# Highway FFN after linear attention: x added on GpSimd, output as fp16 transposes in pairs, weights 0.5(w_h - I), pairwise query sums, whole-batch exps

## Chip, cores and metric

One core of one Trainium2 chip. The metric is device time in microseconds (us). Engines: PE = TensorE matmul, PEld = TensorE weight load, DVE = VectorE, ACT = ScalarE, POOL = GpSimd, SP = SyncE. Every kernel here ran once with a profile and some rounds without, in turn with the kernel before on the same chip. Runs of a higher time at a lower granted TensorE clock are marked slow. Results are right unless "wrong on purpose" is said.

## Reference, cut

```python
# q, k, v: (8 batches, 8 heads, 576, 64) fp32; 0.1 * randn
q_s = softmax(q, axis=-1)                  # over the head dimension
k_s = softmax(k, axis=2)                   # over the sequence
kv  = einsum('bhsd,bhse->bhde', k_s, v)
x   = einsum('bhsd,bhde->bhse', q_s, kv).transpose(0, 2, 1, 3).reshape(4608, 512)
H   = maximum(x @ w_h, 0)
T   = sigmoid(x @ w_t + b_t)
out = T * H + (1 - T) * x                  # (4608, 512) fp32
```

## The kernel before: the parts concerned

Work is issued by hand in numbered positions, eight for each batch. An engine's instructions are queued in the order of issue. x and the gated term g are kept transposed (features on partitions) as fp16; an output tile turns 128 tokens back and is copied out of PSUM as fp32. Names in the profile: `eq`, `ek` are exp(q), exp(k); `psk` is k^T v with the column of sums; `rz`, `kvn` its reciprocal and normalised form; `r` the query sums; `pq`, `qsT` the query transposes; `px`, `xT` the attention output; `pt`, `ph` the two FFN products; `dd` and `g` the blend; `nat`, `o` the output tiles.

```python
def cast_weight(n, k_, eng):               # w_h: four slices, POOL and ACT in turn
    o, i = w16[n][:, k_], w32[n][:, k_]
    eng.copy(o, i) if eng is nc.scalar else eng.tensor_copy(o, i)

def q_sums(b, a):                          # two halves of a batch
    h = slice(2 * a, 2 * a + 2)
    nc.vector.reduce_sum(qsum[b][:, :, h], eq[b][:, :, h, :], axis=AX.X)

def q_scale_p(b, n0, n1):                  # the "products": eq times 1/sum, on POOL
    e, r = eq[b][:, n0:n1], qsum[b][:, n0:n1]
    nc.gpsimd.tensor_mul(e, e, r.broadcast_to(list(e.shape)))

def carry(c, ob):                          # ... four matmuls x @ w_h into ps
    nc.vector.scalar_tensor_tensor(dd, ps, 0.0, xv(ob), op0=ALU.max, op1=ALU.subtract)

def blend(c, ob):                          # th = tanh: T = 0.5 (1 + th)
    nc.vector.scalar_tensor_tensor(gv(ob), th, 1.0, dd, op0=ALU.add, op1=ALU.mult)

def turn_block(t, k_, xs, us):             # x + 0.5 g, turned back by two matmuls
    mm(t[:, k_, :], xs, ident, True, False)
    mm(t[:, k_, :], us, half_i, False, True)
# out_tile: 4 turn_blocks = 8 matmuls for 512 columns of fp32 in PSUM, one copy
...
    if b > 2:
        s = p + {3: -2, 4: -4}.get(b, -5)              # p = 8 * (b - 1)
        at(s, E(exp_half, b, "q", 0))
        at(s + 1, E(exp_half, b, "q", 1), E(q_sums, b, 0))
        at(s + 2, E(q_sums, b, 1), E(q_recip, b))
        if b > 3:
            at(s + 2, E(q_scale_p, b, 0, 4))
            at(s + 3, E(q_scale_p, b, 4, N9))
        s = p + {3: 0, 4: 0}.get(b, -1)
        at(s, E(exp_half, b, "k", 0), E(cast_v, b, 0))         # v casts: POOL
        at(s + 1, E(exp_half, b, "k", 1), E(cast_v, b, 1))
```

The softmax here doesn't subtract the row's maximum and nothing guards it: scores larger than these inputs give would overflow.

Of the kernel before, what the change touches and what calls it, by code (L numbers as in the profile page):

```python
# [18 lines left out]
def kernel(  # L19
# [10 lines left out]
    nc = tc.nc  # L30
# [74 lines left out]

    def cast_weight(n, k_, eng):
        o, i = w16[n][:, k_], w32[n][:, k_]
        if eng is nc.scalar:
            eng.copy(o, i)
        else:  # L110
            eng.tensor_copy(o, i)

    for w in "qkv":
        load(0, w, [nc.sync, nc.sync])
# [35 lines left out]
    def exp_half(b, which, a):  # L150
# [6 lines left out]
            AF.Exp,  # L157
        )

    def cast_v(b, a, eng=None):  # L160
        (eng or nc.gpsimd).tensor_copy(  # L161
            v16s[b % 2][:, :, 2 * a : 2 * a + 2, 0:64],
            in32["v"][b][:, 2 * a : 2 * a + 2].rearrange("p c n d -> p n c d"),
        )
# [30 lines left out]
    def q_sums(b, a):  # L195
        if a == 0:
            qsum[b] = small.tile([P, N9, 4], FP32, tag="r32", name=f"r32_{b}")
        h = slice(2 * a, 2 * a + 2)
        nc.vector.reduce_sum(qsum[b][:, :, h], eq[b][:, :, h, :], axis=AX.X)  # L199

    NG = [(0, 4), (4, 8), (8, 9)]

# [88 lines left out]
    def carry(c, ob):  # L291
        xv = views(c)[0]
        ps = ps_ht.tile([P, 8, 64], FP32, tag="ht", name=f"ph_{c}_{ob}")
        for k_ in range(4):
            mm(ps, w16["h"][:, k_, ob * P : ob * P + P], xv(k_), k_ == 0, k_ == 3)
        dd = mo.tile([P, 8, 64], FP16, tag="dd", name=f"dd_{c}_{ob}")
        nc.vector.scalar_tensor_tensor(  # L297
            dd, ps, 0.0, xv(ob), op0=ALU.max, op1=ALU.subtract
        )
        live[c, ob] = (live[c, ob], dd)  # L300

# [5 lines left out]
        )  # L307


    o32 = {}  # L310
    rows = out.rearrange("(g p n) m -> g p n m", g=B // 2, n=N9)

    def turn_block(t, k_, xs, us):
        dst = t[:, k_, :]
        mm(dst, xs, ident, True, False)
        mm(dst, us, half_i, False, True)

    def flat(t):
        return t.rearrange("p k d -> p (k d)")

    def out_tile(g, n, spare=False):
        if n % 4 == 0:
            o32[g, n // 4] = og.tile([P, 4, 512], FP32, tag="o32", name=f"o32_{g}_{n}")
        ps, tag = (ps_q, "qx") if spare and n % 4 < 3 else (ps_nat, "nat")
        t = ps.tile([P, 4, P], FP32, tag=tag, name=f"nat_{g}_{n}")
        for k_ in range(4):
            turn_block(
                t, k_,
                xT[g][:, k_, n].rearrange("p b d -> p (b d)"),
                gT[g][:, k_, n].rearrange("p b d -> p (b d)"),  # L330
            )
        o = o32[g, n // 4][:, n % 4, :]
        if spare and n % 2:
            nc.vector.tensor_copy(o, flat(t))
        else:
            nc.scalar.copy(o, flat(t))  # L336
        if n % 4 == 3:
            i = n // 4
            nc.sync.dma_start(rows[g][:, 4 * i : 4 * i + 4, :], o32[g, i])


    rows9 = out.rearrange("(g p n) m -> n p g m", g=B // 2, n=N9)[NM]
# [30 lines left out]
    def at(p, *fs):  # L373
        events.setdefault(p, []).extend(fs)
# [8 lines left out]
    for c in range(1, B + 1):  # L383
        for ob in range(4):
            at(8 * c + 2 * ob + 2, E(blend, c, ob))

    for g in range(B // 2):
        p = 16 * (g + 1)
        if g < B // 2 - 1:
            for i in range(8):  # L390
                at(p + 2 + 2 * i, E(out_tile, g, i))
        else:
            for i in range(8):
                at(p + 1 + i // 2, E(out_tile, g, i, True))
    at(8 * B + 8, E(most9), E(last9))

    at(8, E(q_sums, 2, 1), E(q_recip, 2), E(cast_v, 2, 0), E(q_scale_p, 2, 0, 4))
# [3 lines left out]
    for b in range(2, B):  # L401
        p = 8 * (b - 1)
        if b > 2:
            s = p + {3: -2, 4: -4}.get(b, -5)
            at(s, E(exp_half, b, "q", 0))
            at(s + 1, E(exp_half, b, "q", 1), E(q_sums, b, 0))
            at(s + 2, E(q_sums, b, 1), E(q_recip, b))
            if b > 3:
                at(s + 2, E(q_scale_p, b, 0, 4))
                at(s + 3, E(q_scale_p, b, 4, N9))  # L410
            s = p + {3: 0, 4: 0}.get(b, -1)
            at(s, E(exp_half, b, "k", 0), E(cast_v, b, 0))
            at(s + 1, E(exp_half, b, "k", 1), E(cast_v, b, 1))
            if b == 3:
                at(p + 1, E(q_scale_p, b, 0, 4), E(q_scale_p, b, 4, N9))
        tr, kv, x = {
            2: ((4, 5, 5), (3, 4), (6, 7, 7)),
            3: ((4, 5, 5), (3, 4), (6, 7, 7)),
            4: ((2, 3, 4), (4, 5), (6, 6, 7)),
        }.get(b, ((2, 3, 4), (3, 4), (5, 6, 7)))  # L420
        for i in range(3):
            at(p + tr[i], E(q_trans, b, i))
        at(p + kv[0], E(kv_half, b, 0))
        at(p + kv[1], E(kv_half, b, 1), E(kv_norm, b))
        at(p + x[0], E(x_pair, b, 0))
        at(p + x[1], E(x_pair, b, 1))
        at(p + x[2], E(x_left, b))
# [3 lines left out]
    for f in [  # L431
# [24 lines left out]
        E(exp_half, 2, "q", 0),  # L456
        E(x_pair, 1, 0), E(x_pair, 1, 1), E(blend, 0, 3), E(x_left, 1),
        E(exp_half, 2, "q", 1), E(q_sums, 2, 0),
    ]:
        f()  # L460
    for p in range(8, 8 * (B + 1) + 1):
# [33 lines left out]
```

## Time and profile before

| | before |
|---|---|
| time, median of 3 runs | 141.33 us (141.2 to 141.46) |
| span of the profiled run | 139.3 us |
| busy: PE, DVE, ACT, POOL | 88%, 76%, 63%, 32% |
| chain that ended last | PE 50%, DVE 29%, ACT 5%, POOL 5% |

The page, the table of stretches, one turn of the chain and the costly groups are shown in the prediction. A "turn" below is the time from the reciprocal of one batch's query sums to that of the next. One group, by shape (line, engine, operation, out<-in, count; busy us, mean ns; idle before it and what ended that):

```profile
L111 POOL CAST w16h<-w32h 128x512 f16<-128x512 f32 x2 | 1.3, 676 | 7.4 <-DMA w32h<-in_moe_w_h_dram 7.4
```

POOL casts its two slices of w_h as soon as the load lands, at 21 us, and nobody waits.

### The profile page before, as it was taken

What the parts mean: (1) busy time and instruction counts of PE and PEld (TensorE: products, weight loads), DVE (VectorE), ACT (ScalarE), POOL (GpSimd) and SP (SyncE); (2) the same over time, 40 slices, a digit from 0 to 9 for tenths busy, and PEclk for the clock granted to TensorE, in tenths of its full rate; (3) what the DMA queues carried; (4) which work ended last, traced back from release to release, by engine and by line L of the source; (5) the groups of instructions that cost most, each with busy time, mean ns of one, the idle gap of its engine ahead of it and who ended that gap; (6) DMA issues with size and microseconds to landing.
All of it is one profiled execution on the core that took longest, in us unless ns stands there. A gap on an engine that the chain in (4) does not pass through costs nothing.

```text
span 139.3 us, 3531 instructions
## 1 busy us (share of the span) xinstructions
PE 122.2 (88%) x1477; PEld 66.4 (48%) x1477; DVE 106.4 (76%) x200; ACT 88.1 (63%) x126; POOL 44.5 (32%) x37
## 2 busy tenths in 40 slices
PE   4979999967978799969979999999899999999920
PEld 1335344432443355535644754565465455577610
DVE  1395289987998799996996889979977675667840
ACT  3651377719931998639978879769773745565310
POOL 2006003500395429049309701960592000000000
PEclk9999999999999999999999999999999999999997
DMA  4999999999999999935999999950061015077745
GB/s 144 370 388 409 396 387 410 412 412 406 411 412 401 411 410 407 411 132 191 287 412 404 300 328 404 401 224 0 5 261 47 0 75 226 0 285 301 296 159 168
DMA packets 16022, 40.06 MB, mean 288 GB/s; under 512 B 644, under 2 KB 1672, under 8 KB 14984
## 3 DMA queue, kind: packets, MB, share of 16 engines
q1 hardware_dynamic: 16008, 39.85, 74.8%
q8 instruction: 11, 0.18, 0.5%
q14 instruction: 3, 0.02, 0.0%
HBM read 30.41 MB, written 9.44 MB: 286 GB/s over the span
## 4 chain that ended last, share of the span: by engine, by line
PE 50%; DVE 29%; ACT 5%; POOL 5%; DMA 3%; issue 3%; SPq 0%; DVEq 0%; POOLq 0%
PE pt L59 14%; PE ph L59 13%; DVE r L199 12%; PE nat L59 8%; POOL eq L216 5%; PE pq L64 4%; DVE g L305 4%; PE psk L59 3%; DMA q<-in_q_dram 3%; DVE dd L297 3%; PE warm L59 3%; ACT eq L154 2%; DVE eq L212 2%; PE px L59 2%; DVE r L204 2%
## 5 line engine op out<-in xcount | busy, mean ns | idle before, releaser
L288 ACT ACTIVATE pt<-pt,bt 128x512 f32<-128x512 f32 x36 | 23.9, 665 | 29.3 <-PE pt L59 29.3
L216 POOL TENSOR_TENSOR eq<-eq,r 128x1024 f16<-128x1024 f16 (+1 forms) x12 | 25.6, 2153 | 30.2 <-DVE r L204 30.2
L59 PE MATMUL pt<-xT,w16t 128*128 128x512 f16 x128 | 33.3, 380 | 2.1 <-DVE xT L257 1.7
L59 PE MATMUL ph<-xT,w16h 128*128 128x512 f16 x128 | 32.8, 380 | 0.0
L297 DVE SCALAR_TENSOR_TENSOR dd<-ph,xT 128x512 f16<-128x512 f32 x32 | 21.8, 682 | 7.6 <-PE ph L59 7.5
L305 DVE SCALAR_TENSOR_TENSOR g<-pt,dd 128x512 f16<-128x512 f32 x36 | 24.5, 681 | 1.8
L199 DVE TENSOR_REDUCE r<-eq 128x18 f32<-128x1152 f16 x16 | 21.4, 1345 | 4.3 <-ACT eq L154 4.3
L161 POOL CAST v<-v 128x1152 f16<-128x1152 f32 x15 | 16.9, 1147 | 22.7 <-DMA v<-in_v_dram 20.9
L154 ACT ACTIVATE eq<-q 128x1152 f16<-128x1152 f32 x16 | 18.5, 1171 | 2.7 <-DMA q<-in_q_dram 2.7
L154 ACT ACTIVATE ek<-k 128x1152 f16<-128x1152 f32 x16 | 18.4, 1170 | 2.1 <-DMA k<-in_k_dram 2.1
L59 PEld LDWEIGHTS <-w16t 128*128 128x128 f16 x144 | 12.6, 97 | 13.3 <-issue 1.1
L59 PE MATMUL nat<-half_i,g 128*128 128x128 f16 x140 | 18.7, 219 | 0.0
L59 PEld LDWEIGHTS <-w16h 128*128 128x128 f16 x144 | 12.4, 98 | 11.8 <-issue 1.4
L336 ACT COPY o<-nat 128x512 f32<-128x512 f32 x28 | 16.6, 594 | 1.7 <-issue 1.1
L255 ACT CAST xT<-px 128x512 f16<-128x512 f32 x24 | 13.4, 593 | 6.3 <-PE px L59 6.2
L59 PE MATMUL nat<-ident,xT 128*128 128x128 f16 x128 | 17.3, 219 | 0.0
L59 PE MATMUL warm<-wide,ident 128*128 128x512 f16 x52 | 15.3, 444 | 1.9 <-DVE wide L140 1.9
L59 PEld LDWEIGHTS <-g 128*128 128x128 f16 x144 | 14.1, 98 | 3.8 <-DVE g L305 0.4
L233 DVE COPY qsT<-pq 128x1024 f16<-128x1024 f16 (+1 forms) x24 | 12.8, 553 | 3.2 <-PE pq L64 3.0
L59 PEld LDWEIGHTS <-xT 128*128 128x128 f16 x128 | 12.5, 98 | 5.5 <-issue 2.6
L64 PE MATMUL pq<-ident,eq 128*128 128x128 f16 x144 | 11.5, 219 | 2.5 <-POOL eq L216 1.4
L64 PEld LDWEIGHTS <-eq 128*128 128x128 f16 x144 | 8.9, 98 | 6.4 <-POOL eq L216 3.1
(43 smaller groups left out, 84.6 us busy)
## 6 DMA issues: line engine op xcount, KB each, us to landing
out_dram<-o SPq DMA_DIRECT2D x8, 1024.0 KB, 4.8
q<-in_q_dram SPq DMA_DIRECT2D x7, 1152.0 KB, 13.3
k<-in_k_dram SPq DMA_DIRECT2D x7, 1152.0 KB, 14.3
v<-in_v_dram SPq DMA_DIRECT2D x6, 1152.0 KB, 14.7
v<-in_v_dram SPq DMA_DIRECT2D x4, 576.0 KB, 10.7
q<-in_q_dram SPq DMA_DIRECT2D x2, 576.0 KB, 4.1
k<-in_k_dram SPq DMA_DIRECT2D x2, 576.0 KB, 7.1
w32t<-in_moe_w_t_dram SPq DMA_DIRECT2D x1, 1024.0 KB, 13.6
```

Of the source, the lines that this page charges most:

```text
L59: mm = lambda o, l, r, st, sp: nc.tensor.matmul(o, l, r, start=st, stop=sp, skip_group_check=True)
L64: nc.tensor.matmul(o, i, ident, is_transpose=True, start=True, stop=True, skip_group_check=True,)
L154: nc.scalar.activation(dst[b][:, :, 2 * a : 2 * a + 2, :], in32[which][b][:, 2 * a : 2 * a + 2].rearrange("p c n d -> p n c d"), AF.Exp,)
L161: (eng or nc.gpsimd).tensor_copy(v16s[b % 2][:, :, 2 * a : 2 * a + 2, 0:64], in32["v"][b][:, 2 * a : 2 * a + 2].rearrange("p c n d -> p n ...
L199: nc.vector.reduce_sum(qsum[b][:, :, h], eq[b][:, :, h, :], axis=AX.X)
L216: nc.gpsimd.tensor_mul(e, e, r.broadcast_to(list(e.shape)))
L233: nc.vector.tensor_copy(qsT[b][:, :, n0:n1, :], t[:, :, 0:w, :])
L255: nc.scalar.copy(dst, t[c])
L288: nc.scalar.activation(ps, ps, AF.Tanh, bias=bt2[:, ob : ob + 1], scale=0.5)
L297: nc.vector.scalar_tensor_tensor(dd, ps, 0.0, xv(ob), op0=ALU.max, op1=ALU.subtract)
L305: nc.vector.scalar_tensor_tensor(gv(ob), th, 1.0, dd, op0=ALU.add, op1=ALU.mult)
L336: nc.scalar.copy(o, flat(t))
```

## The change

Five parts. **Weights**: relu(h) - x = max(h, 0) - x is rewritten so that the matmul gives 0.5 (h - x), with 0.5 (w_h - I) as the weight; dd = max(-0.5 x, 0.5 (h - x)), and the 0.5 of the gate is in dd already. **x on POOL**: g + x is formed on POOL instead of by the second matmul of each block. **Pairs**: g + x is then one fp16 tensor, so an output tile is 4 transposes, two tiles share a PSUM bank, and one copy takes both. **Sums**: a batch's query sums by two halving fp16 adds and a short reduction, instead of two long reductions. **Exps**: one exp for a batch instead of two halves, for batches 3 to 7. PE loses 128 small matmuls; POOL gains 32 adds.

```diff
 def cast_weight(n, k_, eng):
+    d = slice(k_ * P, k_ * P + P)                       # for w_h only
+    nc.vector.tensor_sub(i[:, d], i[:, d], ident)
-    eng.copy(o, i) / eng.tensor_copy(o, i)
+    eng.mul(o, i, 0.5) / eng.tensor_scalar_mul(o, i, 0.5)
+def exp_all(b, which): ...                              # one activation, 2304 columns
+def q_sums_all(b):
+    nc.vector.tensor_add(t32, e[:, :, 0:32], e[:, :, 32:64])
+    nc.vector.tensor_add(t16, t32[:, :, 0:16], t32[:, :, 16:32])
+    nc.vector.reduce_sum(qsum[b].rearrange("p n c -> p (n c)"), t16, axis=AX.X)
-    dd, ps, 0.0, xv(ob), op0=ALU.max, op1=ALU.subtract
+    dd, xv(ob), -0.5, ps, op0=ALU.mult, op1=ALU.max
+def add_x(c, ob):
+    nc.gpsimd.tensor_add(gv(ob), gv(ob), xv(ob))
-def out_tile(g, n, ...): ...                            # 8 matmuls, fp32, 1 tile
+def out_pair(g, i, ...): ...                            # 8 transposes, fp16, 2 tiles, one copy
...
             at(8 * c + 2 * ob + 2, E(blend, c, ob))
+            if c < B:
+                at(8 * c + 2 * ob + 3, E(add_x, c, ob))
...
-                at(p + 2 + 2 * i, E(out_tile, g, i))    # p = 16 * (g + 1)
+                at(p + 3 + 4 * i, E(out_pair, g, i))
...
-            at(s, E(exp_half, b, "q", 0))
-            at(s + 1, E(exp_half, b, "q", 1), E(q_sums, b, 0))
-            at(s + 2, E(q_sums, b, 1), E(q_recip, b))
+            at(s, E(exp_all, b, "q"))
+            at(s + 1, E(q_sums_all, b))
+            at(s + 2, E(q_recip, b))
```

More of the change, by code (lines that the diff above doesn't have):

```diff
@@ L107, in cast_weight @@
         o, i = w16[n][:, k_], w32[n][:, k_]
+        if n == "t":
+            eng.tensor_copy(o, i)
+            return
+        d = slice(k_ * P, k_ * P + P)
+        nc.vector.tensor_sub(i[:, d], i[:, d], ident)
         if eng is nc.scalar:
-            eng.copy(o, i)
+            eng.mul(o, i, 0.5)
         else:
-            eng.tensor_copy(o, i)
+            eng.tensor_scalar_mul(o, i, 0.5)
     for w in "qkv":
@@ L158, in exp_half, with exp_all @@
         )
+    def exp_all(b, which):
+        dst, p_ = {"k": (ek, ekp), "q": (eq, eqp)}[which]
+        dst[b] = p_.tile([P, N9, 4, 64], FP16, tag="e", name=f"e{which}_{b}")
+        nc.scalar.activation(
+            dst[b], in32[which][b].rearrange("p c n d -> p n c d"), AF.Exp
+        )
     def cast_v(b, a, eng=None):
@@ L199, in q_sums @@
         nc.vector.reduce_sum(qsum[b][:, :, h], eq[b][:, :, h, :], axis=AX.X)
+    t32 = consts.tile([P, N9 * 4, 32], FP16, name="t32")
+    t16 = consts.tile([P, N9 * 4, 16], FP16, name="t16")
+    def q_sums_all(b):
+        qsum[b] = small.tile([P, N9, 4], FP32, tag="r32", name=f"r32_{b}")
+        e = eq[b].rearrange("p n c d -> p (n c) d")
+        nc.vector.tensor_add(t32, e[:, :, 0:32], e[:, :, 32:64])
+        nc.vector.tensor_add(t16, t32[:, :, 0:16], t32[:, :, 16:32])
+        nc.vector.reduce_sum(
+            qsum[b].rearrange("p n c -> p (n c)"), t16, axis=AX.X
+        )
     NG = [(0, 4), (4, 8), (8, 9)]
@@ L307, in blend @@
         )
+    def add_x(c, ob):
+        xv, gv = views(c)
+        nc.gpsimd.tensor_add(gv(ob), gv(ob), xv(ob))
     o32 = {}
@@ L315, in turn_block, with out_pair @@
         mm(dst, xs, ident, True, False)
-        mm(dst, us, half_i, False, True)
+        mm(dst, us, ident, False, True)
     def flat(t):
         return t.rearrange("p k d -> p (k d)")
-    def out_tile(g, n, spare=False):
-        if n % 4 == 0:
-            o32[g, n // 4] = og.tile([P, 4, 512], FP32, tag="o32", name=f"o32_{g}_{n}")
-        ps, tag = (ps_q, "qx") if spare and n % 4 < 3 else (ps_nat, "nat")
-        t = ps.tile([P, 4, P], FP32, tag=tag, name=f"nat_{g}_{n}")
-        for k_ in range(4):
-            turn_block(
-                t, k_,
-                xT[g][:, k_, n].rearrange("p b d -> p (b d)"),
-                gT[g][:, k_, n].rearrange("p b d -> p (b d)"),
-            )
-        o = o32[g, n // 4][:, n % 4, :]
-        if spare and n % 2:
-            nc.vector.tensor_copy(o, flat(t))
-        else:
-            nc.scalar.copy(o, flat(t))
-        if n % 4 == 3:
-            i = n // 4
-            nc.sync.dma_start(rows[g][:, 4 * i : 4 * i + 4, :], o32[g, i])
+    def out_pair(g, i, spare=False):
+        if i % 2 == 0:
+            o32[g, i // 2] = og.tile([P, 4, 512], FP32, tag="o32", name=f"o32_{g}_{i}")
+        ps, tag = (ps_q, "qx") if spare and i < 3 else (ps_nat, "nat")
+        t = ps.tile([P, 2, 512], FP16, tag=tag, name=f"nat_{g}_{i}")
+        for j in range(2):
+            for k_ in range(4):
+                ptrans(
+                    t[:, j, k_ * P : k_ * P + P],
+                    gT[g][:, k_, 2 * i + j].rearrange("p b d -> p (b d)"),
+                )
+        h = i // 2
+        o = o32[g, h][:, 2 * (i % 2) : 2 * (i % 2) + 2, :]
+        if spare and i % 2:
+            nc.vector.tensor_copy(o, t)
+        else:
+            nc.scalar.copy(o, t)
+        if i % 2:
+            nc.sync.dma_start(rows[g][:, 4 * h : 4 * h + 4, :], o32[g, h])
     rows9 = out.rearrange("(g p n) m -> n p g m", g=B // 2, n=N9)[NM]
@@ L385 @@
             at(8 * c + 2 * ob + 2, E(blend, c, ob))
+            if c < B:
+                at(8 * c + 2 * ob + 3, E(add_x, c, ob))
     for g in range(B // 2):
         p = 16 * (g + 1)
-        if g < B // 2 - 1:
-            for i in range(8):
-                at(p + 2 + 2 * i, E(out_tile, g, i))
-        else:
-            for i in range(8):
-                at(p + 1 + i // 2, E(out_tile, g, i, True))
+        for i in range(4):
+            if g < B // 2 - 1:
+                at(p + 3 + 4 * i, E(out_pair, g, i))
+            else:
+                at(p + 3 + i, E(out_pair, g, i, True))
     at(8 * B + 8, E(most9), E(last9))
@@ L411 @@
             s = p + {3: 0, 4: 0}.get(b, -1)
-            at(s, E(exp_half, b, "k", 0), E(cast_v, b, 0))
-            at(s + 1, E(exp_half, b, "k", 1), E(cast_v, b, 1))
+            at(s, E(exp_all, b, "k"), E(cast_v, b, 0))
+            at(s + 1, E(cast_v, b, 1))
             if b == 3:
@@ L458 @@
         E(exp_half, 2, "q", 1), E(q_sums, 2, 0),
+        *[E(add_x, 0, ob) for ob in range(4)],
     ]:
```

## The prediction

> **What bounds the kernel now.** I read, in this order: the page (busy shares, slices, chain shares), the table of stretches, the chain of waits in order of time, the groups by shape, and the timelines of VectorE (DVE), ScalarE (ACT) and GpSimd (POOL). The page names no single bound:
>
> ```profile
> span 139.3 us, 3531 instructions
> PE 122.2 (88%) x1477; PEld 66.4 (48%) x1477; DVE 106.4 (76%) x200; ACT 88.1 (63%) x126; POOL 44.5 (32%) x37
> PE 50%; DVE 29%; ACT 5%; POOL 5%; DMA 3%; issue 3%; SPq 0%; DVEq 0%; POOLq 0%
> ```
>
> The table of stretches shows why; its columns are PE, weight loads, DVE, ACT, POOL, granted clock, DMA share, GB/s:
>
> ```profile
> 20.00:30.00 10.00, 8.59 (x86) 4.40 (x85) 9.57 (x19) 5.24 (x7) 3.60 (x4) 1.00 1.04 412
> 90.00:100.00 10.00, 9.57 (x154) 5.42 (x152) 8.89 (x17) 8.15 (x13) 3.80 (x4) 1.00 0.25 101
> 110.00:120.00 10.00, 10.00 (x81) 5.46 (x78) 6.53 (x11) 5.71 (x11) 0.00 (x0) 1.00 0.26 105
> ```
>
> To about 62 us DVE sets the pace (9.57 of 10 us in 20 to 30), from 100 us PE alone does, and between them the two take turns. One turn of 12.57 us, in the chain of waits (start, us, what):
>
> ```profile
> 82.23 0.46 DVE kvn L188 x2
> 82.68 1.26 DVE r L199
> 83.94 0.60 DVE dd L297
> 84.54 1.27 DVE r L199
> 85.83 0.38 DVE r L204
> 86.21 0.55 DVE g L305
> 86.76 0.61 DVE xT L257
> 87.40 0.38 PE pt L59
> 87.78 0.45 PE nat L59 x8
> ...
> 92.16 0.41 PE psk L59 x36
> ...
> 94.09 0.48 PE psk L59 x36
> ```
>
> Seen here: 5.4 us of DVE (the normalised kv product, two query sums r, reciprocal, xT) and then 7.1 us of PE up to the second psk. An output tile (nat) costs PE 0.45 us. POOL is off this path and has large gaps, but not with much room: in POOL's timeline the first half of the v cast ends at 91.67 us, and the psk that reads it starts at 92.16.
>
> **What the Trainium skill says.**
> 1. "SBUF — State Buffer", section "Who interferes with whom": a DVE instruction with two SBUF inputs, or in a two-port mode, and a GpSimd instruction that reads SBUF exclude each other for a whole instruction. The trace agrees: the one DVE cast of v (39.96 us) fell across two POOL products and the second of these took 2777 ns, while the same shape at 51 us took 2330.
> 2. "GPSIMD Engine Reference", section 3.1: two-input work on GpSimd pays about 2.6 cycles an element, which at its 1.2 GHz is 2.2 ns. The trace shows 1900 ns for 1024 elements and 2330 for 1280: 1.7 to 1.9 ns each, a little better.
> 3. "VectorE: DVE Perf Modes", section "The perf-mode tier table": tensor_tensor runs 2x on 16-bit SBUF data, tensor_reduce only 1x. The trace: 692 and 824 ns for 1024 and 1280 elements (0.52 ns each plus 164), against 1345 ns for a sum over 1152.
> 4. "PSUM — Partial Sum Buffer", specifications: a transpose writes its input type into PSUM. So two tiles of 512 fp16 fit one 2 KiB bank. The query transposes already do this, 8 in 0.45 us, the same as 8 output matmuls.
>
> The groups that carry the costs:
>
> ```profile
> L216 POOL TENSOR_TENSOR eq<-eq,r 128x1280 f16<-128x1280 f16 x6 | 14.4, 2406 | 0.0
> L216 POOL TENSOR_TENSOR eq<-eq,r 128x1024 f16<-128x1024 f16 x6 | 11.4, 1900 | 30.2 <-DVE r L204 30.2
> L199 DVE TENSOR_REDUCE r<-eq 128x18 f32<-128x1152 f16 x16 | 21.4, 1345 | 4.3 <-ACT eq L154 4.3
> L336 ACT COPY o<-nat 128x512 f32<-128x512 f32 x28 | 16.6, 594 | 1.7 <-issue 1.1
> ```
>
> **The change, part by part.**
>
> *Output tiles.* 32 tiles of 8 matmuls become 16 pairs of 8 transposes: PE saves 16 x 0.45 = 7.2 us busy. ACT copies of 256, 384 and 512 elements took 372, 480 and 594 ns, so 1024 is about 1.03 us for a pair, against two of 0.59; little is gained. On the path the saving counts where PE is it: after the last psk (107.07 us) there are 14 tiles, which become 7 pairs: 7 x 0.45 = **-3.1 us**.
>
> *Query sums, batches 3 to 7.* By the slopes above: add of 1152 0.76 us, of 576 0.46 us, sum of 576 about 0.75 us; starts overlap by some 0.08, so 1.75 against 2.53 us: -0.78 us each, four of the five inside a turn. Both adds have two SBUF inputs, so they can be held by POOL.
>
> *Whole-batch exps.* Two took 2.22 us start to end; one should take some 2.1. About -0.1 each, but it holds tanh or an xT copy up to 1 us longer. Nothing on the path, save at batch 3 below.
>
> *x on POOL.* 32 adds of 512 elements, by the POOL slope about 1.0 us each: POOL goes from 44.5 to some 77 us busy. PE must now wait for the last add of a chunk before its first output pair. The dd and g operations keep their operand kinds and their 680 ns.
>
> *Weights.* Before the first carry DVE gets four 128x128 fp32 subtractions (about 0.3 us each), and ACT and POOL then scale the slices.
>
> Now along the path:
>
> *Start.* Before, w_h was cast at 21.3 to 22.6 us, beside DVE work, and the first dd started at 25.05. The order of the changed kernel puts the subtractions after the eq products, which end at 25.12. They end near 26, POOL's two scalings (676 ns each) and ACT's two near 27.1; only then comes the first ph's last quarter, and dd near 27.6. ACT's tanh stands behind its scalings too. The qsT copies and psk follow: I take **+2.2 us** (DVE idles a part of it, so not all 2.5).
>
> *Batch 3.* POOL's order becomes: add of chunk 1's last block, second half of the v cast, then the query products. The add waits for g (49.67 before), so the products start some 1.3 us later though the sum is earlier; the whole exp also delays an xT copy by 1 us. **+1.1.**
>
> *Batch 4.* Gain of the sum against POOL's longer row: **0.**
>
> *Batches 5 and 7.* This is the step I trust most. After the reciprocal POOL runs: products 4.2, add 1.0, v casts 2.2, and only then the add of the previous chunk's last block 1.0, so 8.5 us. PE runs pt, ph, pt, pq, ph and reaches the first pair of the new group 4.6 us after the reciprocal in batch 7 (86.21 to 87.78, plus 3 us, by the same spacing): it waits some 3.9 us. Then pair 0.45, pq 0.45, psk 0.41, pt 0.97, pq 0.11, psk 0.41: second psk done at 11.3, before at 8.3 (98.78 to 107.07): **+3.0** in batch 7. In batch 5 the same count gives 11.4 against 9.4, less the sum's saving of 0.7: **+1.3.**
>
> *Batch 6.* PE meets the v cast: products 4.2, add 1.0, half cast 1.1, so 6.4 against 5.5 without: the tiles' saving is eaten, the sum's stays, and its adds may wait for POOL adds: **+0.2.**
>
> *End.* The last pair is copied by DVE (about 1.2 us, by 424, 550 and 692 ns for 256, 384 and 512) between the last blends, and the last large store leaves about 2 us later relative to the last matmul, with 1 MB taking 4.8 us to land: **+0.5 to 1.**
>
> Sum: 2.2 + 1.1 + 0 + 1.3 + 0.2 + 3.0 - 3.1 + 0.7 = +5.4, so 146.7 us. I lean back from it, since every stall is estimated from one ordering and a tuned kernel may hide some: **145.5 us**.
>
> **Rivals.**
> 1. *The savings arrive, POOL stays hidden.* For: POOL was 32% busy, the added work is spread, and PE and DVE, which form 79% of the chain, both lose work. If only the start cost stays (+2) and each turn gets 1.5 us shorter (three turns), with -3.1 in the tail: 141.3 + 2 - 4.5 - 3.1 = about 136. Against: the POOL queue is in order, and the adds stand behind 6.4 us of products and casts.
> 2. *Gain and loss cancel.* The stalls of batches 5 and 7 are there, but the start is hidden and sums pay fully: 141.3 + 4.3 - 3.1 - 2.4 + 1 = about 141. For: the two largest terms are of equal size. Against: at the start DVE is busy 9.57 of 10 us.
> 3. *Worse than the sum.* The lock makes both adds of each sum wait for a POOL add (about 1 us each, five batches), and PE's pauses of 4 us lower its clock. 146.7 + 3 to 5 = about 151. The clock was 1.00 in all stretches but the end, so no run here shows how long a pause it stands.
>
> **Range and chances.** The cases weigh about 0.1, 0.25, 0.5 (my sum) and 0.15. The range is 141.0 to 150.0: a term off by one us in two or three places. Under 138.5 (faster by over 2%): 0.11. From 138.5 to 144.2: 0.27. Above: 0.62.
>
> **What would show it.** Start: the first dd near 27.6 instead of 25.05, with PE waiting for w16h on POOL or ACT. Batches 5 and 7: weight loads of g waiting 3 to 4 us for POOL's add, twice; in batch 3 well under that. POOL adds near 1.0 us, POOL near 77 us busy. Sum adds near 0.76 and 0.46 us, longer where they meet POOL. Tail: from the last psk to the last ph 21 us instead of 24. I am wrong if the POOL add runs in about half a microsecond, if PE reaches the pairs late anyway because DVE holds it, or if the start delay vanishes in a wait that I did not see.

## The result

The changed kernel took **155.58 us** (median of 4 runs, 155.31 to 158.48; the one of 158.48 is slow) against 141.28 before in the same rounds: ratio 1.1004, 95% interval 1.0978 to 1.103. A ratio is the mean time of one kernel's fast runs over that of the other's of the same rounds, so not quite the ratio of the medians. It was slower, as predicted, but by 14 us and not by 4: outside the stated range of 141 to 150.

The page of the kernel after, with the row of the granted clock in 40 slices:

```profile
span 153.3 us, 3294 instructions
PE 120.8 (79%) x1349; PEld 60.7 (40%) x1349; DVE 106.8 (70%) x207; ACT 86.1 (56%) x102; POOL 83.3 (54%) x69
PEclk9995999779999999999999699999999879999998
PE 35%; POOL 25%; DVE 20%; issue 7%; ACT 6%; DMA 3%; SPq 0%; POOLq 0%; DVEq 0%; ACTq 0%
```

No engine became the bound: none is busier than 79%. But POOL, 5% of the chain before, is 25% of it now. It is a wait for POOL and not its load. The clock fell in four places. PE saved only 1.4 us of busy time of the 7.2 that the fewer matmuls should give, as its other matmuls ran slower in those places (pt: 392 ns each in the mean, 380 before; ph 401 and 380).

Three stretches of after (the columns as in the prediction: PE, PEld, DVE, ACT, POOL, clock, DMA share, GB/s):

```profile
20.00:30.00 10.00, 5.78 (x27) 2.15 (x24) 7.72 (x17) 4.13 (x6) 2.60 (x2) 0.95 1.05 392
80.00:90.00 10.00, 7.67 (x51) 3.85 (x52) 6.41 (x15) 5.85 (x8) 8.50 (x7) 0.83 0.47 163
110.00:120.00 10.00, 5.01 (x41) 2.63 (x40) 6.35 (x13) 4.25 (x4) 8.84 (x7) 1.00 0.26 106
```

In 20 to 30 neither DVE (9.57 before) nor PE (8.59) is full. In 110 to 120, where PE had been busy without a gap, it is busy for half the time while POOL is busy for 8.84 us.

*Where the time went*, by milestones in the two traces (start times, us): the reciprocal of batch n's query sums is "recip n", that of the last psk "psk 7".

| up to | before | after | shift | added here | predicted |
|---|---|---|---|---|---|
| recip 1 | 22.86 | 24.83 | +2.0 | +2.0 | none |
| first dd | 25.05 | 31.65 | +6.6 | +4.6 | +2.2 (start) |
| recip 2 | 37.73 | 44.34 | +6.6 | 0 | |
| recip 4 | 60.43 | 68.70 | +8.3 | +1.7 | +1.1 (batch 3) |
| recip 5 | 72.25 | 81.73 | +9.5 | +1.2 | 0 (batch 4) |
| recip 6 | 85.83 | 97.09 | +11.3 | +1.8 | +1.3 (batch 5) |
| recip 7 | 98.40 | 110.62 | +12.2 | +1.0 | +0.2 (batch 6) |
| psk 7 | 107.12 | 123.74 | +16.6 | +4.4 | +3.0 (batch 7) |
| last dd | 131.12 | 145.29 | +14.2 | -2.4 | -3.1 (tail) |
| end of span | 139.3 | 153.3 | +14.0 | -0.2 | +0.7 |

*Start.* The chain of waits (start, us, what), first of before, then of after:

```profile
24.30 0.82 DVE eq L212
25.13 0.61 DVE dd L297
```

```profile
26.28 0.82 DVE eq L238
27.11 0.21 DVE w32h L113
27.40 3.13 POOL w16h L117 x2
30.58 2.36 PE ph L59 x6
```

Before, the first dd follows the DVE work directly. After, DVE's subtractions, then two scalings on POOL and the first ph, the latter at a low clock, stand between. The scalings ran in 1482 and 1665 ns, where the plain cast of the same shape took 676.

*A turn with the pairs at its beginning* (batch 7). POOL's timeline of before: products as soon as the reciprocal is there, then two v casts, and nothing else:

```profile
98.95 4.19 POOL L216 TENSOR_TENSOR eq<-eq,r 128x1024 f16<-128x1024 f16 x2 [6.20 <-DVE r L204]
103.09 2.24 POOL L161 CAST v<-v 128x1152 f16<-128x1152 f32 x2
```

Chain of after:

```profile
113.02 2.33 POOL eq L242
115.35 0.17 POOL g L338
...
116.40 2.23 POOL v L174 x2
118.64 1.12 POOL g L338
...
119.80 0.45 PE nat L64 x5
...
121.11 1.74 PE pt L59 x4
```

PE waits for the add of the last block of the previous chunk, which stands in POOL's queue behind products, another add and two v casts. PE's own timeline puts the pause at 3.06 us, and the next pt takes 1.74 us instead of 0.97: the clock fell.

*Query sums*, timeline of DVE (start, us, instruction, and in brackets the idle time before it), first of before, where kvn stands between the two halves:

```profile
68.42 1.34 DVE L199 TENSOR_REDUCE r<-eq 128x18 f32<-128x1152 f16 x1
...
70.47 0.49 DVE L188 TENSOR_TENSOR kvn<-psk,rz 128x128 f16<-128x128 f32 x2
70.88 1.34 DVE L199 TENSOR_REDUCE r<-eq 128x18 f32<-128x1152 f16 x1
```

Then of after, with two of POOL's adds of that time:

```profile
77.22 1.21 DVE L221 TENSOR_TENSOR t<-eq 128x1152 f16<-128x1152 f16 x1 [0.49 <-ACT eq L169]
78.47 1.29 DVE L222 TENSOR_TENSOR t<-t 128x576 f16<-128x576 f16 x1
...
81.13 0.23 DVE L199 RECIPROCAL rz<-psk 128x2 f32<-128x2 f32 x2
81.33 0.49 DVE L201 TENSOR_TENSOR kvn<-psk,rz 128x128 f16<-128x128 f32 x2
```

```profile
77.79 2.98 POOL L338 TENSOR_TENSOR g<-g,xT 128x512 f16<-128x512 f16 x2
```

Two things are seen. The adds last 1.21 and 1.29 us where 0.76 and 0.46 were predicted: POOL was at work. And batch 5's whole sum stands in DVE's queue *before* rz and kvn of batch 4, for which PE is waiting. Over the five batches, by shape:

```profile
L338 POOL TENSOR_TENSOR g<-g,xT 128x512 f16<-128x512 f16 x32 | 37.8, 1190 | 19.9 <-DVE g L331 19.8
L221 DVE TENSOR_TENSOR t<-eq 128x1152 f16<-128x1152 f16 x5 | 5.3, 1056 | 1.0 <-ACT eq L169 1.0
L222 DVE TENSOR_TENSOR t<-t 128x576 f16<-128x576 f16 x5 | 4.0, 791 | 0.2
```

### The profile page after: what moved, and what is told of

Same layout as the page of the kernel before. It is cut to its first block, busy times and chain, and to the rows that moved or that the text cites. A ratio compares the mean times of both kernels' runs of the same rounds, so it can differ in the third digit from the quotient of the medians.

```text
span 153.3 us, 3294 instructions
## 1 busy us (share of the span) xinstructions
PE 120.8 (79%) x1349; PEld 60.7 (40%) x1349; DVE 106.8 (70%) x207; ACT 86.1 (56%) x102; POOL 83.3 (54%) x69
## 4 chain that ended last, share of the span: by engine, by line
PE 35%; POOL 25%; DVE 20%; issue 7%; ACT 6%; DMA 3%; SPq 0%; POOLq 0%; DVEq 0%; ACTq 0%
POOL eq L242 12%; PE pt L59 10%; PE ph L59 10%; POOL g L338 5%; POOL v L174 5%; DVE r L212 4%; PE warm L59 3%; DMA q<-in_q_dram 3%; PE nat L64 3%; PE psk L59 3%; PE pq L64 3%; ACT eq L160 2%; PE px L59 2%; DVE t L221 2%; POOL w16h L117 2%
## 5 line engine op out<-in xcount | busy, mean ns | idle before, releaser
L338 POOL TENSOR_TENSOR g<-g,xT 128x512 f16<-128x512 f16 x32 | 37.8, 1190 | 19.9 <-DVE g L331 19.8
L59 PE MATMUL ph<-xT,w16h 128*128 128x512 f16 x128 | 35.3, 401 | 4.6 <-POOL w16h L117 4.6
L242 POOL TENSOR_TENSOR eq<-eq,r 128x1024 f16<-128x1024 f16 (+1 forms) x12 | 25.6, 2153 | 11.1 <-DVE r L230 7.4
L323 DVE SCALAR_TENSOR_TENSOR dd<-xT,ph 128x512 f16<-128x512 f16 x32 | 21.7, 678 | 9.9 <-PE ph L59 9.8
L368 ACT CAST o<-nat 128x1024 f32<-128x1024 f16 x14 | 14.2, 1012 | 14.0 <-PE nat L64 12.8
L64 PE MATMUL nat<-ident,g 128*128 128x128 f16 x128 | 10.9, 225 | 3.8 <-POOL g L338 3.7
L64 PEld LDWEIGHTS <-g 128*128 128x128 f16 x128 | 8.9, 101 | 8.5 <-POOL g L338 4.4
L212 DVE TENSOR_REDUCE r<-eq 128x18 f32<-128x1152 f16 x6 | 8.0, 1349 | 4.7 <-ACT eq L160 4.7
L169 ACT ACTIVATE eq<-q 128x2304 f16<-128x2304 f32 x5 | 10.6, 2128 | 0.0
L169 ACT ACTIVATE ek<-k 128x2304 f16<-128x2304 f32 x5 | 10.6, 2122 | 0.0
L117 POOL TENSOR_SCALAR w16h<-w32h 128x512 f16<-128x512 f32 x2 | 3.1, 1574 | 13.4 <-DVE w32h L113 13.4
## 6 DMA issues: line engine op xcount, KB each, us to landing
v<-in_v_dram SPq DMA_DIRECT2D x4, 576.0 KB, 11.3
```

The costliest lines, as they stand in the source:

```text
L59: mm = lambda o, l, r, st, sp: nc.tensor.matmul(o, l, r, start=st, stop=sp, skip_group_check=True)
L64: nc.tensor.matmul(o, i, ident, is_transpose=True, start=True, stop=True, skip_group_check=True,)
L169: nc.scalar.activation(dst[b], in32[which][b].rearrange("p c n d -> p n c d"), AF.Exp)
L323: nc.vector.scalar_tensor_tensor(dd, xv(ob), -0.5, ps, op0=ALU.mult, op1=ALU.max)
L338: nc.gpsimd.tensor_add(gv(ob), gv(ob), xv(ob))
L368: nc.scalar.copy(o, t)
```

## The experiments

Theory after the result: the cost is the *place in the queue* of the added work (adds ahead of v casts and products on POOL, weight work behind DVE's, a sum ahead of kvn). Rivals: the *amount* of POOL work and its holding of DVE; the fallen clock; the operations themselves. The first four runs add one part to the kernel before (141.3 us in the same rounds; 141.4 to 141.5 in the later ones).

| run | us, median | ratio to before (fast runs) |
|---|---|---|
| p1_weights | 147.93 | 1.0464 [1.0381, 1.0547] |
| p2_sums | 143.01 | 1.0117 [1.0100, 1.0134] |
| p3_exps | 141.59 | 1.0039 [0.9999, 1.0079] |
| p4_xpool (wrong) | 149.47; the fast one 146.15 | none: one fast run |
| u1_scale_dve | 154.66 | 1.0963 |
| u2_pairs_later | 152.86 | 1.0769 |
| u3_dead_add (wrong) | 150.59 | 1.0633 |
| u4_no_add (wrong) | 143.82; the fast one 140.37 | none: one fast run |
| v1_weights_early | 141.51 | 0.9995 [0.9958, 1.0031] |
| v2_sums_late | 142.19 | 1.0025 [0.9971, 1.0079] |
| v3_casts_first (wrong) | 139.24 | 0.9832 [0.9794, 0.9870] |
| v4_fill | 154.59 | 1.0889 |
| w2_v1_v3 | 140.26 | 0.9892 [0.9826, 0.9958] |
| w1_best | **136.39** | **0.9656 [0.9626, 0.9687]** |
| w4_add3_later | 137.67 | 0.9726 [0.9679, 0.9774] |
| w3_all_reordered | 140.42 | 0.9942 [0.9913, 0.9971] |

A caution: the profiles of after, p1, u2 and u4 have a dip of the clock during warm-up, ahead of everything that was changed, and reach recip 1 by 1.4 to 2.9 us later than before; those of u1, u3, v4 and the others have none. Whether a run without a profile has it, no trace shows. Where such runs are compared, the stretch from recip 1 to the last dd in the two profiles is given as well: 108.3 us in before, 120.5 in after.

### p1_weights: the weights part alone, on the kernel before

```diff
+        nc.vector.tensor_sub(i[:, d], i[:, d], ident)
+        eng.mul(o, i, 0.5) / eng.tensor_scalar_mul(o, i, 0.5)     # ACT / POOL
-            dd, ps, 0.0, xv(ob), op0=ALU.max, op1=ALU.subtract
+            dd, xv(ob), -0.5, ps, op0=ALU.mult, op1=ALU.max
-        mm(dst, us, half_i, False, True)
+        mm(dst, us, ident, False, True)
```

> The kernel before with one part of the change alone: weights 0.5(w_h - I), the new form of dd, and ident in place of half_i in the output matmuls. Right result. My theory: the start is paid in full and never won back, because the chain from 25 to 62 us is a chain of compute; in the changed kernel's trace the two POOL scalings took 1574 ns each where the plain casts took 676, and the first dd came 4.6 us later than the shift already there. So about +4.5 us (145.8), with the first dd near 29.5 to 30 us and nothing lost after that. Rival: the start hides under the loads, which run at 390 GB/s until 60 us, and the loss is all later: then within 1 us of 141.3.

147.93 us, more than expected. The first dd started at 30.94 us, and from there on every milestone stayed 5.9 us late to the end. 1.4 us of it came before any changed instruction (below). POOL's scalings took 1490 ns each, one of them with DVE idle, so that is their own time and no holding. The start costs about 4.5 us, not 2.2, and none of it is hidden later (recip 1 to the last dd: 112.7 us, 4.5 more than before).

### p2_sums: pairwise sums alone

```diff
-            at(s + 1, E(exp_half, b, "q", 1), E(q_sums, b, 0))
-            at(s + 2, E(q_sums, b, 1), E(q_recip, b))
+            at(s + 1, E(exp_half, b, "q", 1), E(q_sums_all, b))
+            at(s + 2, E(q_recip, b))
```

> The kernel before with the pairwise fp16 sums for batches 3 to 7 alone. Right result. My theory: without POOL's 32 adds the two DVE adds meet POOL only when it casts or scales, so they take 0.76 and 0.46 us (in the changed kernel they took 1056 and 791 ns in the mean) and each of the turns of batches 5, 6 and 7 gets shorter by about 0.8 us, unless POOL's v cast then ends too late for psk: -1.5 to -2.5 us (139 to 140). Rival: the sums lose by themselves (two extra instructions, waits between them): 0 to +1 us.

A miss: 143.01 us, slower than before, although the adds took 756 and 458 ns as predicted. DVE idled 3.7 us, four times, before them: the first half of the sum used to run while ACT made the second half's exp; the pairwise sum waits for both. What a turn gained in the sum it lost there. And in batch 5 the sum stands before kvn of batch 4; PE's timeline has that wait (the profiled run was a slow one, so the wait and not the time after it is the evidence):

```profile
73.50 0.62 PE L59 MATMUL px<-qsT,kvn 64*64 64x512 f16 x5 [1.76 <-DVE kvn L188]
```

### p3_exps: whole-batch exps alone

```diff
-            at(s, E(exp_half, b, "q", 0))
-            at(s + 1, E(exp_half, b, "q", 1), E(q_sums, b, 0))
+            at(s, E(exp_all, b, "q"))
+            at(s + 1, E(q_sums, b, 0))          # k likewise
```

> The kernel before with whole-batch exps for batches 3 to 7 alone. Right result. My theory: off the path, save at batch 3 where an xT copy waits behind one exp of 2.1 us: 0 to +1 us. Rival: ScalarE's longer instruction holds up tanh and with it PE's next tiles in every turn: +2 to +4 us.

141.59 us: off the path, as predicted.

### p4_xpool: x on POOL and the pairs alone (wrong: the old weights give x + 2 T (H - x))

```diff
+    at(8 * c + 2 * ob + 3, E(add_x, c, ob))
-    at(p + 2 + 2 * i, E(out_tile, g, i))
+    at(p + 3 + 4 * i, E(out_pair, g, i))
```

> The kernel before with x added on GpSimd and the output tiles as fp16 transposes copied two at a time, nothing else. The weights are the old ones, so the result is WRONG on purpose (x + 2T(H-x) for x + T(H-x)); every instruction has the shape it has in the changed kernel. My theory: this is the larger part of the loss; POOL's row of products, adds and casts makes PE wait in batches 5 and 7, and in the others for the v cast, and the clock falls after the pauses: +4 to +7 us (145.5 to 148.5). Rival: the loss comes from the lock between DVE's two-input sums and POOL's adds; then this part alone, whose DVE work has no sums of two SBUF inputs, is faster than before by the 3 us of the tail.

146.15 us in the profiled run at clock 0.98, as expected; 149 to 152 in three runs at 0.95 to 0.96, which are marked slow. By the one fast run this part costs 4.8 us, about as much as the weights (4.5 without the dip). The four ratios (1.034 here, of one run) multiply to 1.099, close to the 1.1004 of all parts together.

### u1_scale_dve: after, with POOL's two scalings on DVE

```diff
-        *[E(cast_weight, "h", k_, (nc.gpsimd, nc.scalar)[k_ % 2]) for k_ in range(4)],
+        *[E(cast_weight, "h", k_, (nc.vector, nc.scalar)[k_ % 2]) for k_ in range(4)],
```

> The changed kernel with one thing undone: the two slices of w_h that POOL scales (1574 ns each) are scaled by DVE instead (a tensor_scalar of this kind should take some 420 ns, as the cast of w_t does). My theory: the start cost is mostly POOL's slow scaling: the first dd comes 2 to 2.5 us earlier and the whole kernel ends that much earlier, some 153 us. Rival: what counts is only that the weights wait behind DVE's queue; then less than 1 us is won.

154.66 us: 0.9 less instead of 2 to 2.5. The first dd came 6.34 us after recip 1, against 6.82 in after, and from recip 1 to the last dd nothing was gained (121.7 us). A faster engine in the same place of the queue helps little. One of the two scalings was itself long, 1.40 us with a POOL v cast beside it; they are still behind the query work.

### u2_pairs_later: after, with all but the last pairs four positions later

```diff
-                at(p + 3 + 4 * i, E(out_pair, g, i))
+                at(p + 7 + 4 * i, E(out_pair, g, i))
```

> The changed kernel with the output pairs of the first three groups issued four positions later (7 + 4i instead of 3 + 4i), so that PE meets the first pair of a group half a chunk after POOL's last add; POOL's own row is untouched. My theory: PE's wait for the last add, about 4 us in batch 7 with the fall of the clock after it, and the smaller ones in batches 3 and 5, goes away, what is left there is a wait for the v cast: -3 to -5 us (150.5 to 152.5). Rival: POOL's row delays psk through the v cast by as much, so the pairs only take the blame: within 1 us of 155.5.

152.86 us (fast runs 151.78 to 153.0): 2.7 less. Its profile fell in a slow run, so only the times count. PE's stalls in front of the pairs are real, but moving the reader leaves POOL's queue as it is.

### u3_dead_add: after, the add's result written to scratch (wrong)

```diff
-        nc.gpsimd.tensor_add(gv(ob), gv(ob), xv(ob))
+        nc.gpsimd.tensor_add(wide.rearrange("p (n d) -> p n d", d=64), gv(ob), xv(ob))
```

> The changed kernel, but POOL's add writes to a scratch tile that nobody reads, so PE transposes the product without x and waits for no add. Result WRONG on purpose; POOL does the same work in the same order. My theory: like the pairs issued later, 150.5 to 152.5. What remains against the run without any add is the cost of POOL's time itself: v casts that come late and DVE's sums held by POOL.

150.59 us: POOL does the same work, PE does not wait for it, and 5 us go. Between the two profiles it is 2.7 us from recip 1 to the last dd (117.8), and 2.0 more are the dip in warm-up, which this one lacks.

### u4_no_add: after, without the adds (wrong)

```diff
-        nc.gpsimd.tensor_add(gv(ob), gv(ob), xv(ob))
+        pass
```

> The changed kernel without the adds of x on POOL at all. Result WRONG on purpose; everything else as in the changed kernel. My theory: the sums' two adds drop to 0.76 and 0.46 us, the v casts follow the products at once, no pair waits: some 8 to 9 us less, 146 to 147.5, that is before plus the start's 6 less the tail's 3 and with nothing from the sums. Rival (the lowered clock has other causes, and POOL is not it): over 150.

143.82 us median, 140.37 in the one fast run (clock 0.972): 7 to 10 us beyond the dead add, more than expected (9.0 us from recip 1 to the last dd by the profiles, of which this one is of a slow run). The sums' adds were back at 757 and 458 ns. So what the adds delay behind them in POOL's queue (v casts, products) and in DVE costs more than PE's direct wait for them. This run can't say whether it is their amount or their place.

### v1_weights_early: p1, with the subtractions on POOL when w_h lands and all scalings on ACT

```diff
-        nc.vector.tensor_sub(i[:, d], i[:, d], ident)
+        nc.gpsimd.tensor_sub(i[:, d], i[:, d], ident)
-        (nc.gpsimd, nc.scalar)[k_ % 2]
+        nc.scalar
```

> The weights part alone on the kernel before (147.9 us with it), but the identity is subtracted by POOL, which idles when w_h lands, and all four slices are scaled by ACT; DVE's queue has no part in it. Right result. In the run before this one (scalings moved to DVE) only 0.6 us of the start came back, because DVE's scalings took 916 ns in the mean beside POOL's casts of v and still stood behind DVE's query products. My theory now: the start cost is the place in DVE's queue together with the slow scaling, so here the first dd comes by 26.3 us (25.05 before) and the kernel runs 141.3 to 142.8 us. Rival: the new form of dd or the ident matmul costs by itself: it stays over 145.

141.51 us, ratio 0.9995: all of p1's cost is gone, with the same arithmetic. The place and the engine changed together here (two scalings went from POOL, 1490 ns, to ACT, 618 ns); u1 shows that a faster engine without the place gains little. Timelines of POOL and ACT in this run:

```profile
21.43 1.84 POOL L113 TENSOR_TENSOR w32h<-w32h,ident 128x128 f32<-128x128 f32 x4 [7.46 <-DMA w32h<-in_moe_w_h_dram]
```

```profile
22.14 2.19 ACT L115 ACTIVATE w16h<-w32h 128x512 f16<-128x512 f32 x4 [1.99 <-POOL w32h L113]
```

Both stand where their engine was idle, and are done at 24.3 us; the first dd starts at 25.31.

### v2_sums_late: p2, with batch 5's sum one position later

```diff
+            at(s + (2 if b == 5 else 1), E(q_sums_all, b))
```

> The sums alone on the kernel before (143.0 us with them), with those of batch 5 put behind the normalised kv product of batch 4 in DVE's queue, where the second half sum stood before the change. Right result. My theory: the loss of 1.7 us is the new wait in batch 5, where one whole sum stands before kvn and waits for both exps while PE waits for kvn (1.8 us in its trace) and loses its clock: here 140.3 to 141.5 us, no slow run. Rival: the sums themselves are the loss (waiting for both exps in each batch): it stays near 143.

142.19 us median, 1.0025, between the theory and its rival: most of p2's loss goes when kvn is ahead of the sum, but there is no gain over before either.

### v3_casts_first: p4, with the v casts of batches 4 to 7 issued before the products (wrong, as p4)

```diff
             if b > 3:
+                at(s, E(cast_v, b, 0))
+                at(s + 1, E(cast_v, b, 1))
                 at(s + 2, E(q_scale_p, b, 0, 4))
...                                                  # and taken out behind the k exps
```

> x on POOL alone on the kernel before (146.2 to 152.0 us with it), with POOL's casts of v of batches 4 to 7 put ahead of the query products, into the time in which POOL waits for the reciprocal. Result WRONG on purpose, as in that run. My theory: it is the order of POOL's queue, not the amount of its work, that costs: with the casts gone from between the products and the last add, the pairs of batches 5 and 7 wait 2.2 us less and no psk waits for a cast: 3 to 5 us less than the run without this, 142.5 to 145. Rival: POOL has simply too much to do (80 us busy): no gain over 1 us.

139.24 us, all runs fast, more gained than expected: 7 us less than p4's one fast run, 10 less than its median, and under the kernel before. Same instructions; only the order on POOL differs. The waits of PE (total us, times, longest), first of p4, then of this run:

```profile
PE nat L64 <- POOL g L312: 6.8, 3, 3.1
```

```profile
PE nat L64 <- POOL g L312: 2.6, 3, 0.9
```

This decides against the rival of POOL's amount: with 80 us of POOL work the kernel is 2 us faster than with 44.

### v4_fill: after, with idle matmuls in three of PE's pauses

```diff
+    E(fill, 16)              # before the first ph
+    for _ in range(10): mm(f_, ident, wide, True, True)    # before the first pair of groups 1 and 2
```

> The changed kernel (155.5 us) with idle matmuls that nobody reads put into three of PE's pauses: 16 before the first carry, 10 before the first pair of the second and of the third group, in a PSUM bank free at that time. Right result. It keeps PE busy and changes no wait. Theory that the fall of the granted clock after a pause is a part of the loss: the clock stays near 1.00 after these pauses and 2 to 4 us come back, 151.5 to 153.5. Rival (the low clock only falls into time in which PE waits anyway): within 1 us of 155.5, or slower by the filling itself, up to 4 us.

154.59 us, clock 0.968 to 0.985 instead of 0.93 to 0.95: 1 us. In its profiled run psk 7 came 12.0 us after recip 7 (13.1 in after, 8.7 in before). This profile lacks the dip in warm-up; from recip 1 to the last dd it took 118.9 us, 1.6 less than after, of which 1.1 in the last turn. So the fallen clock is worth 1 to 1.6 us, as the rival had it: a consequence of the waits and a small part of the loss. One pause, of 2.35 us before PE's px of batch 4, was not filled; the clock stayed up after it here and fell in after, by luck as far as the traces tell.

### w2_v1_v3: v1 and v3 together, a right result

```diff
# the weights part as in v1_weights_early, the POOL part as in v3_casts_first
```

> Weights with the identity subtracted early by GpSimd and scaled by ACT, plus x added on GpSimd with output pairs and the v casts of batches 4 to 7 put before the query products; a right result. If the two mends are independent their ratios multiply: 0.9995 (weights early) times 0.983 (casts first) is 0.983, so about 139.0 us. If instead the early subtractions (some 2 us of GpSimd in the prologue) push the first adds and products back, 141 or more.

140.26 us (138.9 to 140.57): 1 us short of the product of the ratios, a miss. PE still waits for POOL's add before the pairs; psk 7 came 11.1 us after recip 7.

### w1_best: w2, with the pairs two positions later

```diff
-                at(p + 3 + 4 * i, E(out_pair, g, i))
+                at(p + 5 + 4 * i, E(out_pair, g, i))
```

> As w2 with the output pairs two positions later, which took 2.7 us off the changed kernel. Casts first left 2.6 us of PE waiting for GpSimd's adds ahead of the pairs and 3.0 us ahead of weight loads. If those waits sat on the path: 137 to 138 us. If they were slack by then (the waits were at most 1 us each): as w2, 139.

**136.39 us**, 3.4% under the kernel before, with a right result. PE leads the chain again. Lines of the page, and a stretch, of this run:

```profile
PE 116.1 (86%) x1349; PEld 59.1 (44%) x1349; DVE 105.7 (78%) x198; ACT 87.6 (65%) x114; POOL 80.6 (60%) x71
PE 51%; DVE 18%; POOL 13%; ACT 5%; issue 4%; DMA 4%; SPq 0%; POOLq 0%; DVEq 0%
```

```profile
110.00:120.00 10.00, 10.00 (x66) 5.29 (x65) 7.27 (x13) 5.65 (x8) 5.73 (x5) 1.00 0.27 107
```

PE's busy time is 6.1 us under that of before, close to the 7.2 of the prediction, and POOL is 60% busy without PE waiting for its adds. POOL's timeline around batch 7:

```profile
93.32 2.24 POOL L168 CAST v<-v 128x1152 f16<-128x1152 f32 x2
95.52 1.16 POOL L319 TENSOR_TENSOR g<-g,xT 128x512 f16<-128x512 f16 x1
97.54 4.19 POOL L223 TENSOR_TENSOR eq<-eq,r 128x1024 f16<-128x1024 f16 x2 [0.86 <-DVE r L211]
101.69 4.47 POOL L319 TENSOR_TENSOR g<-g,xT 128x512 f16<-128x512 f16 x4
```

The casts and an add run before the products, in what was idle time, and nothing but products is between the reciprocal and the query transposes.

### w4_add3_later: w1, with the fourth add of each batch one position later

```diff
-                at(8 * c + 2 * ob + 3, E(add_x, c, ob))
+                at(8 * c + 2 * ob + 3 + ob // 3, E(add_x, c, ob))
```

> As w1 with the add of the fourth block of every batch one position later, so that in batch 3 the second v cast and the query products stand before the add that waits for DVE. Batch 3's products started 1.0 us after the recip of its sums in the casts-first run, where they start 0.5 us after it in the kernel before: theory, up to 0.5 to 1 us less than w1; rival, that batch 3's psk and not its products set its end: same as w1.

137.67 us, 0.7% slower than w1: a miss. In batch 3 the products did start sooner (51.39 us against 52.14), but two adds then ran between them and batch 4's v casts, and batch 4's products began at 62.26 us against 61.63.

### w3_all_reordered: the changed kernel, all five parts, with the queues mended

```diff
# after, with: the subtractions on POOL and scalings on ACT (v1), v casts before the
# products for batches 4 to 7 (v3), pairs two positions and the fourth add one position
# later (w4), batch 5's sum after kvn (v2)
```

> The changed kernel with all its five parts and only the order of queues mended: subtractions early on GpSimd, all four scalings on ACT, v casts before the products for batches 4 to 7, fourth add and pairs later, batch 5's sum after kvn. A right result. Theory, that order was the cause: as w4 plus what the sums and whole exps cost when mended (ratio 1.0025 and 1.0039, some 1 us), so 138.5 to 141 us against 155.6. Rival, that holding of DVE's sums by GpSimd and the mere amount of its work cost time by themselves: 144 or more, with the sum's adds over 1.0 us.

140.42 us with a right result: 15 us less than the changed kernel, and within 1% of the kernel before. All five parts are in it, so the loss came from where their work stood in the queues, together with the engines chosen for the weight work, and not from the parts as such. It is 2.8 us behind w4, which has the same order without pairwise sums and whole exps. By shape, the sums' adds in w3:

```profile
L221 DVE TENSOR_TENSOR t<-eq 128x1152 f16<-128x1152 f16 x5 | 5.6, 1116 | 0.5 <-ACT eq L169 0.5
L222 DVE TENSOR_TENSOR t<-t 128x576 f16<-128x576 f16 x5 | 4.8, 952 | 0.2
```

With the reduction of 753 ns a sum is 2.8 us, which is no less than the two reductions of 1346 that it replaces: with POOL busy, the pairwise sum has nothing left to gain. So the rival of holding was right on that part. Some of the 2.8 us may be clock: w3's profile has it at 0.50 around 50 to 52 and 64 to 65 us, w4's has it only at the end.

## Why the prediction was wrong

The direction, the places and most mechanisms were right: PE waits for POOL's adds at batches 5 and 7, DVE is held, the start is late, the tail is shorter. The sum was +5.4 and the traces show +14.0. What failed is the pricing: added work was given its own duration, or that of a similar operation, and not what its place in the queue makes wait. The 8.6 us beyond the sum are, rounded: start 2.4, warm-up 2.0, batch 7 1.4, batch 4 1.2, batch 6 0.8, tail 0.7, batch 3 0.6, batch 5 0.5; the end gave 0.9 back. By its steps:

- **"POOL's two scalings (676 ns each)"**: the failed step of the start. The duration was taken from the plain cast; the scaled form took 1482 and 1665 ns (1490 in p1). PE, idle meanwhile, had its granted clock at 0.50 (29.05 to 30.6 us), and the first ph took longer for it. The start was +4.6 and not +2.2. "DVE idles a part of it, so not all 2.5" was a discount with no reason in the profile; p1 shows that the delay stays to the last microsecond.
- **"Batch 4: 0"** was +1.2, and batch 6 was +1.0 and not +0.2. I priced the sums by their durations alone and did not look at where they stand. In batch 4's turn the whole sum of batch 5 stands before kvn, waits for both exps and is held by POOL; PE waited 2.35 us there (p2 and v2 show the place without POOL's part in it). In batch 6's turn the sum of batch 7 was held: its adds took 1.24 and 1.29 us beside three of POOL's adds, so the stretch from the last psk to recip 7 took 4.54 us, where it was to shrink from 3.84 by 0.8. Adds "longer where they meet POOL" was said in words and given no number in the sum: they took 1.85 us together and not 1.22.
- **Batch 3: +1.1**, measured +1.7. The mechanism was right: add, half cast, then products, which started at 59.81 us, 2.4 after recip 3 (0.5 before).
- **Batch 7: +3.0**, measured +4.4; batch 5: +1.3, measured +1.8. POOL's row "products 4.2, add 1.0, v casts 2.2, add 1.0", 8.5 us, took 8.6. With the steps between engines PE went on 8.8 us after the reciprocal's end, 0.3 more than reckoned, and the work after its pause ran at a low clock (pt 1.74 us and not 0.97, psk 0.64 and not 0.41), 1.1 us more. Filling the pauses took 1.1 us away.
- **Tail -3.1**, measured -2.4: from the last psk to the last dd 21.6 us, before 24.0; the prediction said 21. **End +0.7**, measured -0.2: the last large store did leave 2 us later relative to the last dd, but the span ends 5 us after the last small store (134.12 us before, 148.28 after), so that delay was hidden.
- **POOL adds near 1.0 us, POOL near 77 us**: 1.19 (1.15 undisturbed) and 83.
- **The lean from 146.7 to 145.5** went the wrong way. Rival 3, the held sums and the fallen clock, was given 0.15, and it was nearest; but its clock part is only 1 to 1.6 us (v4), and its size (151) left the doubled start out.
- **Not in the prediction**: 2.0 us of the shift come before the first changed instruction, 1.6 of them from a low clock (0.50) at 12 to 14 us, during warm-up. The profiles of after, p1, u2 and u4 have such a dip, the other fourteen don't. It follows a pause of PE before the first query transposes, which was 2.08 to 3.03 us long in those four and 0.72 to 2.08 in the others. PE's timelines of before and of after:

```profile
9.93 0.61 PE L64 MATMUL pq<-ident,eq 128*128 128x128 f16 x8 [0.77 <-DVE r L210]
```

```profile
10.29 0.61 PE L64 MATMUL pq<-ident,eq 128*128 128x128 f16 x8 [2.34 <-DVE r L236]
```

  The changes do not touch that stretch. All four are among the seven profiles that keep the weight work late; whether that has a part in it stays open.

The larger mistake is of kind: "it costs what the ordering gives" was taken as fixed. Rival 1's time was there to be had (w1, which leaves the sums and exps out: 136.39; its estimate 136), but only once the v casts went ahead of the products and the weight work to where engines were idle.

What stays open: how the 2.8 us between w4 and w3 divide into sums, exps and clock, and why some pauses of PE lower the clock and others of the same length don't.

## What to carry to other kernels

Moving work to an idle engine pays or costs by its *place in that engine's queue*: list what the path waits for on that engine (here products and v casts) and put the new work behind it, or the old work earlier, before judging the engine. An instruction that joins two halves waits for both inputs, and one that is shorter by itself need not be shorter beside another engine's work (a sum's second add took 0.46 us alone, 0.95 in w3). Take a duration only from the same operation, not from one of the same shape.

## What the Trainium skill lacked or had wrong

- "GPSIMD Engine Reference", section 4.1, calls one-input work roughly line-rate. It does not tell a cast from a scaled cast: 128x512 from fp32 to fp16 took 624 to 676 ns as a cast and 1482 to 1665 ns times 0.5. ACT took 618 ns for the same scaling.
- The same page's 2.6 cycles an element for two inputs (section 3.1, for fp32) fits fp16 adds: 1150 ns for 512 columns, 2.2 ns each. The products with a broadcast operand, 1.8 to 1.9 ns, are better than the page has it.
- "SBUF — State Buffer", section "Who interferes with whom": agrees. What it does not give is the size for a short DVE instruction: the add of 576 took 458 ns alone and up to 1.29 us beside POOL, 0.95 on average in w3.
- "TensorE: Matmul & The Clock Gate", section "What's actually happening", has the clock low after at least one idle window of about 3.4 us. Here shorter pauses of PE were followed by a low clock: 1.76 us (p2), 2.08 (p1), 2.10 (u4), 2.34, 2.35 and 3.06 (after; ph 1.60 us and pt 1.74, both about 1 otherwise). Others were not: 2.01 and 2.90 us (p4), 2.08 (v3), 2.35 (v4). So in this range the length alone does not decide. The page's free-running window may bear on it, but no run here shows that. In this kernel, which waits anyway, filling three pauses gained about 1 us of 155 (v4).
